# Top-32 attention and a capacity-limited mixture of experts: rearranging both ends of the kernel

## The chip, the cores and the metric

The kernel runs on one core of one Trainium2 chip. The metric is the device time of one execution in microseconds; lower is better. The core has a matrix engine (PE, with its weight loads shown as PEld), a vector engine (DVE), a scalar engine (ACT), a general engine (POOL), a queue that only issues transfers (SP), and sixteen DMA engines. Each engine works through its own list of instructions in order and waits on semaphores for the others. PE writes its results to PSUM, eight banks of 128 x 512 fp32; the other data lie in SBUF, and inputs and outputs in DRAM.

## The reference

Attention over 8 batches, 8 heads, 576 positions and head size 64, where each row of scores keeps its 32 largest entries; its output, as 4608 tokens of 512 numbers, goes through eight experts, each token to the one with the largest logit, and each expert keeps the 80 tokens with the largest gate.

```python
def _attn_ref(q, k, v):
    scores = scale * np.matmul(q, k.transpose(0, 1, 3, 2))
    kth = np.partition(scores, -top_k, axis=-1)[..., -top_k:-top_k + 1]
    scores = np.where(scores >= kth, scores, -1000000000.0)
    attn = np.exp(scores - np.max(scores, axis=-1, keepdims=True))
    attn = attn / (np.sum(attn, axis=-1, keepdims=True) + 1e-09)
    return np.matmul(attn, v)

def _moe_ref(x, w_gate, w1, w2, capacity):
    logits = x @ w_gate
    expert_idx = np.argmax(logits, axis=1)
    probs = softmax(logits)
    gate_w = probs[np.arange(N), expert_idx]
    out = np.zeros((N, D))
    for e in range(E):
        tok_idx = np.where(expert_idx == e)[0]
        if len(tok_idx) > capacity:
            keep = np.argpartition(-gate_w[tok_idx], capacity)[:capacity]
            tok_idx = tok_idx[keep]
        h = np.maximum(x[tok_idx] @ w1[e], 0.0)
        out[tok_idx] = gate_w[tok_idx, None] * (h @ w2[e])
    return out
```

Sizes of the second part: w1 is 8 x 512 x 1024, w2 is 8 x 1024 x 512.

## The kernel before

**Attention.** Work comes in 32 pairs of heads (`n`). `load` brings a pair's q, k and v; `turn` transposes q and k on PE (ten transposes into the four-bank score tile `sp`, which `four()` hands out and of which there is only one) and ACT copies the two halves to `qT` and `kT` (L189). A pair has five tiles of rows (`t`), four of 128 rows and a last one of 64 in which both heads share the partitions. A *unit* is one tile of one head: nine units a pair, 288 in all. For a tile, `front` multiplies q by k into `sp` (L201) and ACT copies the scores to `s` (L206). For a unit, DVE searches the 32nd largest score of every row: `parts` takes maxima of six stretches (L213), `search` takes maxima of those (L224, L232), ACT counts signs against the 24th (L229), DVE or, for odd units, POOL multiplies scores by signs (L236), DVE takes another maximum (L238) and picks the threshold (L241). `below` makes a mask (L250 on ACT, L254 on POOL or, for the last unit, DVE). `turn_w` transposes scores and adds masks on PE into `ab` (two banks, one buffer) and `cc` (L286, L291), and ACT takes the exponentials into `wT` (L293, L295). `back` multiplies by v (L309), `over` takes reciprocals of the sums (DVE, L321), `divide` scales into `xn` (ACT, L330).

**The order.** `run` writes the order out by hand: `step(i)` interleaves the searches of units i to i-4, then `turn_w` of the tile ended by unit i-4, the divisions, `front` of the tile that begins with unit i+4, `back` of the tile ended by unit i-5, and, where no front was issued, `turn` of the next pair. Steps run from -4 on.

**After a pair.** `norm` writes `xn` to DRAM (`xd`, two transfers, L336 and L337), transposes it into a score tile (L178, L179), copies it to `xT` (L342), multiplies it by the gate's weights in another score tile (twenty small matmuls, L347), copies the 40 logits of each row out (L353) and adds them up over the four pairs of a batch (L356). After every second batch `gates` makes the gate weights on DVE (L367 to L390) into `R`. `norm` is a generator: each `yield` puts its next part into a later step.

**Routing.** `route` first makes fixed matrices on POOL and DVE (L597 to L625: `emask`, `same`, `ahead`, `ofe`, `ones`, `col`, `base`). Then it transposes `R` (L637), takes the 24 largest of each group (L647 to L657), merges them (L653), searches the 80 largest of each expert (L669, L671), and builds lists of tokens with PE (`acc`, L701). `warm(n)` issues n idle 128x128 by 256 bf16 matmuls on zeros (L632): 100 after the merge (WARM1), 36 after `acc` (WARM2).

**Experts.** `finish` loads the weights of expert 4, calls `route`, makes two lists of indices on DVE (`idx_x` for reading, L722, `idx_s` for writing, L725 and L727), and runs eight experts in a pipeline. `gather` reads 80 rows of `xd` by an indirect DMA of POOL (L740), `turn_g` transposes them (L750, copied by DVE, L752), `hidden` makes the hidden layer (128 matmuls, L763, two copies with ReLU on ACT, L765), `product` multiplies by w2 (128 matmuls in one PSUM bank `yp`, L776, copied by ACT after each half, L779), `store` transposes back (L785), scales (DVE, L787) and writes rows to `out` by an indirect DMA of POOL (L788). In round e the order is `hidden(e)`, `store(e-2)`, `product(e-1)`, loads of weights, `gather(e+3)`, `turn_g(e+2)`. `judge` checks that the fast search was exact; otherwise a second, plain path would run, which it does not here.

Of the kernel before, what the change touches and what calls it, by code (L numbers as in the profile page):

```python
# [11 lines left out]
I32 = mybir.dt.int32  # L12
# [15 lines left out]
def kernel(  # L28
# [33 lines left out]
    WARM1, WARM2 = 100, 36  # L62
# [40 lines left out]
    nc.scalar.mul(huge, ident, -HUGE)  # L103

# [22 lines left out]
    class Attention:  # L127
# [47 lines left out]
        def turn_in(self, ps, t):  # L175

            for c in range(NF):
                nc.tensor.transpose(ps[:, c * P : (c + 1) * P], t[:, c, :], ident)  # L178
            nc.tensor.transpose(ps[:, NF * P : S], t[:TL, NF, :], ident[:TL, :TL])  # L179

        def turn(self, n):

            four = self.four()
            ps = [four[:, 2 * j : 2 * j + 2, :].rearrange("p j c -> p (j c)") for j in range(2)]
            for j, src in enumerate(self.qk.pop(n)):
                self.turn_in(ps[j], src.rearrange("p c h d -> p c (h d)"))
            self.turned[n] = [self.qkp.tile([P, S], F32, name=name, tag=name) for name in ("qT", "kT")]
            for j in range(2):
                nc.scalar.copy(self.turned[n][j], ps[j][:, :S])  # L189

        def front(self, n, t):
# [14 lines left out]
            nc.scalar.activation(s[:, : g * S].rearrange("p (j c) -> p j c", c=HS), ps[:, : 2 * g, :HS], Act.Copy, scale=TINY)  # L206
# [67 lines left out]
        def turn_w(self, n, t):  # L274
# [3 lines left out]
            ab = self.ps_w.tile([P, 2, NF, P], F32, name="ab", tag="ab")  # L278
# [53 lines left out]
        def norm(self, n, b, hp, bi, nb):  # L332

            xn = self.xn.pop(n).rearrange("p c h d -> p c (h d)")
            ones, cols = bass.ds(b, 1), slice(hp * P, (hp + 1) * P)
            nc.sync.dma_start(xv[ones, : NF * P, cols].rearrange("o (c p) d -> p (o c) d", p=P), xn[:, :NF, :])  # L336
            nc.sync.dma_start(xv[ones, NF * P :, cols].rearrange("o p d -> p o d"), xn[:TL, NF:, :])  # L337
            yield 1
            ps = self.four()[:, :2, :].rearrange("p j c -> p (j c)")
            self.turn_in(ps, xn)  # L340
            xT = self.xT
            nc.scalar.copy(xT[:, :S], ps[:, :S])  # L342
            yield 1
            lp = self.four()[:, 0, : NK * E].rearrange("p (c e) -> p c e", e=E)
            for c in range(NK):
# [5 lines left out]
            lg = self.lg[:, bi]  # L351
            part = lg if hp == 0 else self.small.tile([P, NK, E], F32, name="part", tag="part", bufs=2)
            nc.scalar.copy(part, lp)  # L353
# [3 lines left out]
            if hp == HP - 1 and bi == nb - 1:  # L357
                yield 0
                yield from self.gates(b - bi, nb)
# [527 lines left out]
```

## Time and profile before

| | us |
|---|---|
| median of 7 runs | 1028.66 (1027.07 to 1030.61) |
| the profiled execution | 1027.55 |
| its span, first to last instruction | 1025.8 |
| busy: PE, DVE, ACT, POOL | 899.4, 895.5, 786.1, 456.0 |
| attention, first search of DVE to last maximum | 12.3 to 880.5 |
| last pair's sums, gates | 880.5 to 893.7 |
| routing up to the first gather | 893.7 to 920.0 |
| experts | 924 to 1025.8 |

The profile gives, for each engine, busy time by source line and output tile, the idle time ahead of a group of instructions and what ended it, the clock that PE was granted (1.0 is full, 0.5 is half), and the chain of waits that ended last. L286 means line 286 of the kernel before. In a timeline a row has the start, the length, the engine, the line, the operation, the output and inputs, and in brackets the idle time of that engine just before, with what released it.

### The profile page before, as it was taken

The page shows a single profiled execution, that of the slowest core. Times are in us where ns is not written, and L with a number is a line of the kernel's source. Part 1 is how long each engine was busy: PE and PEld are TensorE (multiplying, and loading weights), DVE is VectorE, ACT ScalarE, POOL GpSimd, SP SyncE. Part 2 cuts the span into 40 slices and gives each one's busy share as a digit, 9 for nine tenths or more (in the row PEclk, how much of TensorE's full clock was granted, in tenths as well). Part 3 has the DMA queues.
Part 4 walks back from the last instruction along what each step waited for, and adds up shares of the span by engine and source line. Part 5 has one row for each costly group of instructions (what it writes and reads, how often), then busy time and mean ns, then how long its engine had stood idle before and what let it go on. Part 6 is the DMA issues. An engine that isn't in the chain of part 4 may idle for free.

```text
span 1025.8 us, 35579 instructions
## 1 busy us (share of the span) xinstructions
PE 899.4 (88%) x13381; PEld 727.0 (71%) x13381; DVE 895.5 (87%) x5087; ACT 786.1 (77%) x1671; POOL 456.0 (44%) x331
## 2 busy tenths in 40 slices
PE   5889999999889999989899999998989998699896
PEld 3677777777667777777677777776777777588786
DVE  3999999999999999999999999999999999551000
ACT  3888899888888998889898888898889888401110
POOL 1544555554454545545454544555455554211101
PEclk9999999999999999999999999999999999879998
DMA  4244443333333333332333311111121200225900
GB/s 93 77 118 130 122 128 89 89 89 89 90 89 87 73 79 79 79 84 81 89 89 89 89 40 44 40 47 48 48 49 48 49 13 14 96 89 201 352 23 24
DMA packets 167893, 85.76 MB, mean 84 GB/s; under 512 B 117792, under 2 KB 154656, under 8 KB 167712
## 3 DMA queue, kind: packets, MB, share of 16 engines
q1 hardware_dynamic: 166688, 80.78, 28.8%
q0 software_dynamic: 1024, 2.62, 0.9%
q8 instruction: 107, 1.75, 0.7%
q14 instruction: 74, 0.61, 0.2%
HBM read 63.19 MB, written 20.19 MB: 81 GB/s over the span
## 4 chain that ended last, share of the span: by engine, by line
DVE 55%; PE 28%; ACT 11%; issue 3%; another core or an unknown queue 1%; DMA 1%; POOL 0%; SPq 0%; POOLq 0%; ACTq 0%; DVEq 0%
DVE cand L213 17%; DVE w L238 12%; PE cc L309 7%; DVE y L236 6%; DVE cand L232 6%; DVE pick L241 4%; DVE top L224 4%; PE yp L776 3%; PE ab L286 3%; PE sp L201 3%; ACT wT L295 3%; PE sp L178 2%; ACT sign L229 2%; DVE w L224 2%; ACT mask L250 1%
## 5 line engine op out<-in xcount | busy, mean ns | idle before, releaser
L213 DVE MAX8 cand<-s 128x8 f32<-128x96 f32 x1728 | 386.7, 243 | 9.5 <-ACT s L206 9.5
L254 POOL TENSOR_SCALAR mask<-s,thr_all 128x576 bf16<-128x576 f32 x159 | 273.7, 1721 | 199.7 <-PE ab L291 135.2
L309 PEld LDWEIGHTS cc<-vb,wT 128*64 128x64 f32 x5760 | 200.3, 138 | 112.6 <-ACT wT L295 95.7
L236 POOL TENSOR_TENSOR y<-s,sign 128x576 f32<-128x576 f32 x128 | 164.0, 1281 | 240.3 <-ACT sign L229 106.4
L309 PE MATMUL cc<-vb,wT 128*64 128x65 f32 x5760 | 222.4, 225 | 53.1 <-ACT wT L295 53.1
L229 ACT ACTIVATE sign<-s,w 128x576 bf16<-128x576 f32 x288 | 225.9, 785 | 46.5 <-DVE w L224 46.2
L238 DVE MAX8 w<-y 128x8 f32<-128x576 f32 x288 | 217.3, 755 | 2.2 <-POOL y L236 2.0
L201 PE MATMUL sp<-kT,qT 64*128 64x288 f32 (+1 forms) x1280 | 202.0, 435 | 14.7 <-ACT part L353 6.1
L286 PE MATMUL ab<-ident,s 128*128 128x128 f32 x1152 | 176.7, 282 | 10.9 <-ACT wT L295 10.9
L206 ACT ACTIVATE s<-sp 128x1152 f32<-128x1152 f32 (+1 forms) x160 | 167.2, 1045 | 11.1 <-PE sp L201 9.5
L286 PEld LDWEIGHTS ab<-ident,s 128*128 128x128 f32 x1152 | 128.5, 142 | 34.6 <-ACT wT L295 25.1
L295 ACT ACTIVATE wT<-ab 128x1024 f32<-128x1024 f32 (+1 forms) x160 | 150.8, 942 | 0.0
L201 PEld LDWEIGHTS sp<-kT,qT 64*128 64x128 f32 (+1 forms) x1280 | 105.5, 179 | 53.3 <-ACT part L353 8.0
L236 DVE TENSOR_TENSOR y<-s,sign 128x576 f32<-128x576 f32 x160 | 118.2, 739 | 3.1 <-ACT sign L229 2.6
L224 DVE MAX8 top<-cand 128x8 f32<-128x48 f32 x576 | 114.2, 198 | 0.1
L291 PEld LDWEIGHTS <-mask 128*128 128x128 bf16 x1440 | 94.5, 98 | 25.7 <-ACT mask L250 19.0
L232 DVE MATCH_REPLACE8 cand<-top,cand 128x48 f32<-128x48 f32 x576 | 109.8, 191 | 0.0
L250 ACT ACTIVATE mask<-s,thr_all 128x576 bf16<-128x576 f32 x128 | 99.5, 777 | 0.3 <-DVE pick L241 0.2
L330 ACT ACTIVATE xn<-cc,z_all 128x64 f32<-128x64 f32 (+1 forms) x320 | 82.8, 316 | 2.3 <-DVE z_all L321 2.3
L241 DVE SCALAR_TENSOR_TENSOR pick<-past,cnt,w 128x9 f32<-128x9 f32 x288 | 82.7, 287 | 0.0
L286 PE MATMUL cc<-ident,s 128*128 128x128 f32 x288 | 79.0, 274 | 0.2 <-ACT xn L330 0.2
L293 ACT ACTIVATE wT<-cc 128x256 f32<-128x256 f32 (+1 forms) x160 | 57.5, 359 | 6.3 <-PE cc L291 4.8
(192 smaller groups left out, 978.1 us busy)
## 6 DMA issues: line engine op xcount, KB each, us to landing
w<-in_moe_w_dram SPq DMA_DIRECT2D x32, 512.0 KB, 4.6
w<-in_moe_w_dram SPq DMA_DIRECT2D x8, 2048.0 KB, 12.5
out_dram<-zero SPq DMA_DIRECT2D x9, 1024.0 KB, 5.9
qn<-in_q_dram SPq DMA_DIRECT2D x64, 128.0 KB, 2.6
kn<-in_k_dram SPq DMA_DIRECT2D x64, 128.0 KB, 2.5
vb<-in_v_dram SPq DMA_DIRECT2D x64, 128.0 KB, 2.6
xd<-xn SPq DMA_DIRECT2D x32, 256.0 KB, 4.2
qn<-in_q_dram SPq DMA_DIRECT2D x32, 32.0 KB, 2.5
```

The lines of the kernel that those rows point to most:

```text
L201: nc.tensor.matmul(o, lhsT=qT[d, t * P : t * P + m], rhs=kT[d, j * HS : (j + 1) * HS], start=True, stop=True)
L206: nc.scalar.activation(s[:, : g * S].rearrange("p (j c) -> p j c", c=HS), ps[:, : 2 * g, :HS], Act.Copy, scale=TINY)
L213: nc.vector.max(out=cand[:, j, :], in_=s[:, j * S // NG : (j + 1) * S // NG])
L224: nc.vector.max(out=dst, in_=cand)
L229: nc.scalar.activation(sign, s, Act.Sign, bias=w9[:, 7:8], scale=-1.0, accum_out=cnt)
L232: nc.vector.match_replace(out=cand, in_to_replace=dst, in_values=cand, imm_value=LOW)
L236: engine.tensor_tensor(out=y, in0=s, in1=sign, op=Alu.mult)
L238: nc.vector.max(out=w9[:, 8:], in_=y)
L254: engine.tensor_scalar(self.mask[i], self.s[i], self.thr[:, i : i + 1], None, op0=Alu.is_lt)
L286: nc.tensor.matmul(dst[h][c], lhsT=sc[:, keys[c]], rhs=ident, start=c == 0 or (c == NF and h == 0), stop=False, is_transpose=True, skip_gr ...
L295: nc.scalar.activation(wT[:, : g * NF, :], ab.rearrange("p h c r -> p (h c) r")[:, : g * NF, :], Act.Exp, scale=scale / TINY)
L309: nc.tensor.matmul(cc[r : r + TL, o], lhsT=wT[:, j * NF + c if c < NF else 2 * NF + j, r0 : r0 + TL], rhs=vb[:, c, h, :], start=(c == 0), ...
```

## The change

The diff, cut to its core; the plain path's buffers (`route_all`) become fewer, which changes nothing that runs.

1. The numbers of idle matmuls go from 100 and 36 to 92 and 14.
2. Fixed matrices are made at the kernel's beginning; `ofe` is dropped, a part of `same` takes its place.
3. `turn` writes one tile for q and k. For the first pair q is copied before k is transposed; for the others one copy moves both.
4. The first tile's scores are copied one head at a time. In steps 0 and 1 `front` looks three units ahead and not four, and the second pair's `turn` isn't allowed in step 0.
5. The last `turn_w` puts its `ab` into the score tile.
6. The last pair goes through `norm` twice, first with four chunks of rows, then with the fifth. The steps in which `norm` no longer waits for a free place begin one step earlier.
7. The buffers of the experts and the PSUM of `turn_g` and `store` are set aside before routing instead of after it. `idx_s` is made after the first three gathers are issued.
8. `product` is copied once as a whole; the last expert's is copied by halves, from two PSUM tiles.

```diff
-    WARM1, WARM2 = 100, 36
+    WARM1, WARM2 = 92, 14
...
+    GB = 2 * B
+    GE = B * E
+    emask = const.tile([P, E], F32, name="emask")
+    nc.vector.tensor_reduce(emask, ident.rearrange("p (g e) -> p e g", e=E), axis=AX, op=Alu.add)
+    same = const.tile([P, GB, E], F32, name="same")
+    nc.vector.tensor_copy(same, emask.unsqueeze(1).to_broadcast([P, GB, E]))
+    ahead = const.tile([P, P], F32, name="ahead")
+    nc.gpsimd.affine_select(out=ahead, in_=same.rearrange("p g e -> p (g e)"), compare_op=Alu.is_gt, fill=0.0, base=0,
+                            pattern=[[1, P]], channel_multiplier=-1)
+    for i in range(2):
+        nc.gpsimd.memset(base[i * GE : (i + 1) * GE, 1:2], float(2 * P if i == 0 else TL // 2))
+    nc.gpsimd.iota(base_i, pattern=[[0, 1]], base=0, channel_multiplier=1)
+    nc.vector.tensor_scalar(base_i, base_i, 3, None, op0=Alu.arith_shift_right)
+    nc.vector.tensor_copy(base[:, 0:1], base_i)
...
+            both = self.qkp.tile([P, 2, S], F32, name="both", tag="both")
+            self.turned[n] = both[:, 0, :], both[:, 1, :]
             for j, src in enumerate(self.qk.pop(n)):
                 self.turn_in(ps[j], src.rearrange("p c h d -> p c (h d)"))
-            self.turned[n] = [self.qkp.tile([P, S], F32, name=name, tag=name) for name in ("qT", "kT")]
-            for j in range(2):
-                nc.scalar.copy(self.turned[n][j], ps[j][:, :S])
+                if n == 0:
+                    nc.scalar.copy(both[:, j, :], ps[j][:, :S])
+            if n > 0:
+                nc.scalar.copy(both, four.rearrange("p (k j) c -> p k (j c)", k=2)[:, :, :S])
...
-            nc.scalar.activation(s[:, : g * S].rearrange("p (j c) -> p j c", c=HS), ps[:, : 2 * g, :HS], Act.Copy, scale=TINY)
+            for j in range(0, 2 * g, 2 if i == 0 else 2 * g):
+                w = 2 if i == 0 else 2 * g
+                nc.scalar.activation(s[:, j * HS : (j + w) * HS].rearrange("p (j c) -> p j c", c=HS), ps[:, j : j + w, :HS],
+                                     Act.Copy, scale=TINY)
...
-            ab = self.ps_w.tile([P, 2, NF, P], F32, name="ab", tag="ab")
+            if i == NU - 1 and not self.lean:
+                ab = self.four().rearrange("p h (c r) -> p h c r", r=P)
+            else:
+                ab = self.ps_w.tile([P, 2, NF, P], F32, name="ab", tag="ab")
...
-        def norm(self, n, b, hp, bi, nb):
+        def norm(self, n, b, hp, bi, nb, cs=range(NK)):
...
+            if full:
+                nc.sync.dma_start(xv[one, : NF * P, cols].rearrange("o (c p) d -> p (o c) d", p=P), xn[:, :NF, :])
+            if NF in cs:
+                nc.sync.dma_start(xv[one, NF * P :, cols].rearrange("o p d -> p o d"), xn[:TL, NF:, :])
             yield 1
             ps = self.four()[:, :2, :].rearrange("p j c -> p (j c)")
-            self.turn_in(ps, xn)
+            at = slice(cs[0] * P, min(S, cs[-1] * P + P))
+            self.turn_in(ps, xn, cs)
-            nc.scalar.copy(xT[:, :S], ps[:, :S])
+            nc.scalar.copy(xT[:, at], ps[:, at])
             yield 1
             lp = self.four()[:, 0, : NK * E].rearrange("p (c e) -> p c e", e=E)
-            for c in range(NK):
+            for c in cs:
...
-                ends = [n for n, t in drawn if t == NF]
+                ends = [(n, range(NK) if n < NP - 1 else range(NF) if t < NF else range(NF, NK))
+                        for n, t in drawn if t == NF or (n == NP - 1 and t == NF - 1)]
...
-                busy = 0 <= i + 4 < NU and units[i + 4][2] != 1
+                f = i + 4 if i not in (0, 1) else i + 3
+                busy = 0 <= f < NU and units[f][2] != 1
                 if busy:
-                    self.front(*units[i + 4][:2])
+                    self.front(*units[f][:2])
...
-                if due and not busy:
+                if due and not busy and i > 0:
...
-                    step(i, i >= NU + 6)
+                    step(i, i >= NU + 5)
...
-            nc.tensor.matmul(few[:, 0:1], lhsT=ofe.rearrange("k g e -> k (g e)"), rhs=bar8, start=True, stop=True)
+            nc.tensor.matmul(few[:, 0:1], lhsT=same[:E, :, :].rearrange("k g e -> k (g e)"), rhs=bar8, start=True, stop=True)
...
+        fs = stack.enter_context(tc.tile_pool(name="fs", bufs=2))
+        ps_x = stack.enter_context(tc.tile_pool(name="ps_x", bufs=2, space=PSUM))
         routing = stack.enter_context(ExitStack())
...
-            ps = ps_y.tile([P, HP, P], F32, name="yp", tag="y")
             y_t[e] = fs.tile([P, HP, cap], F32, name="yT", tag="yT")
+            step = HP if e < E - 1 else HP // 2
             for d in range(HP):
+                if d % step == 0:
+                    ps = ps_y.tile([P, HP, P], F32, name="yp", tag="y")
...
-                if d % 2:
-                    nc.scalar.copy(y_t[e][:, d - 1 : d + 1, :], ps[:, d - 1 : d + 1, :cap])
+                if d % step == step - 1:
+                    nc.scalar.copy(y_t[e][:, d + 1 - step : d + 1, :], ps[:, d + 1 - step : d + 1, :cap])
...
             for e in range(3):
                 gather(e)
+            em = sl.tile([cap, E], F32, name="em")
+            nc.vector.tensor_scalar(em, i1, 0.0, float(4 * N), op0=Alu.is_equal, op1=Alu.mult)
+            idx_s = sl.tile([cap, E], I32, name="idx_s")
+            nc.vector.scalar_tensor_tensor(out=idx_s, in0=i1, scalar=-1.0, in1=em, op0=Alu.add, op1=Alu.add)
```

## The prediction

> **What bounds the kernel now.** I read the 40 slices first, then stretches of 100 us, then the chain of waits through the end, then the timelines of the first 32 us and from 866 us on.
>
> ```profile
> DVE  3999999999999999999999999999999999551000
> PEclk9999999999999999999999999999999999879998
> 760.00:860.00 100.00, 90.53 (x1312) 72.10 (x1309) 100.00 (x581) 90.95 (x193) 50.83 (x34) 1.00 0.13 32
> ```
>
> The third line is one stretch of the attention (length, then busy us of PE, PEld, DVE, ACT, POOL, then clock): DVE is busy for all of it, PE and ACT for 91 of 100. So from 30 to 866 us the program is DVE's list, and an edit that spares ACT there (one copy in `turn` instead of two) moves nothing. The change can earn only where DVE is not full: the first 30 us, the drain from 866 to 894, the routing to 924, the experts to the end. The experts, by the chain of waits:
>
> ```profile
> 945.38 0.44 ACT hT L765
> 945.82 4.12 another core or an unknown queue
> 949.97 0.30 ACT yT L779
> 950.27 0.04 issue
> 950.32 2.43 PE yp L776 x64
> ...
> 984.94 2.56 PE yp L776 x64
> 987.58 0.30 ACT yT L779
> ```
>
> Between the halves of each product PE stands still for ACT's copy of the first half: both halves share one PSUM tile. For experts 1, 2 and 3 the copy is released late as well: 4.12, 4.08 and 4.04 us after the piece before, where other first halves take 2.24 to 2.57. POOL's timeline names the only thing special there, a scatter and a gather back to back; each late copy starts 0.7 to 0.8 us after that pair ends:
>
> ```profile
> 947.04 0.95 POOL L788 DMA_INDIRECT out_dram<-y,idx_s  x1 [20.24 <-DVE y L787]
> 948.29 0.97 POOL L740 DMA_INDIRECT xg<-xd,idx_x  x1 [0.30 <-issue]
> ```
>
> **Experts.** Eight products, first yp matmul to the next other matmul: 5.14, 6.78, 6.85, 8.18, 5.41, 5.25, 5.42, 5.41, together 48.44 us. `hidden` runs the same 128 matmuls (64 at a time, 128x80 out) without a stop in 4.42 us (930.64 to 935.06), 4.58 when a transpose follows. Eight at 4.58, one of them at 4.42, are 36.5, so 11.9 us go. Within it, 1.45 is a clock drop in expert 3 (below), about 1.5 each is the late release of experts 1 to 3 (4.4), the rest the plain stop, 0.6 to 0.85 a product. The last expert keeps half copies but in two PSUM tiles, so it loses its stop too. The whole copy is 320 columns; the row of that size is L765, 0.44 us, against 0.29. It hides behind the next transposes and `hidden` (5 us before `store` reads yT), except in the last round, where `store(6)` follows `product(6)` directly: now 0.97 us from matmul to matmul (two transposes overlap the second copy), then about 0.26+0.44+0.04+0.56 = 1.30. Cost 0.3. Sum: -11.6. If the late release is not tied to POOL and PE only waits elsewhere, 4.4 and the clock drop stay: -5.7.
>
> **Drain.** The last turn of weights (L286, unit 287) waits for ACT to empty `ab`:
>
> ```profile
> 883.88 0.66 PE L286 MATMUL ab<-ident,s 128*128 128x128 f32 x4 [1.23 <-ACT wT L295]
> 888.58 0.64 ACT L342 COPY xT<-sp 128x576 f32<-128x576 f32 x1 [0.36 <-PE sp L179]
> 891.62 0.38 DVE L598 TENSOR_REDUCE emask<-ident 128x8 f32<-128x128 f32 x1 [0.23 <-POOL base L619]
> ```
>
> In the score tile, free since 876.74, it starts at 882.5 and ends at 883.5, under that copy; the 60 matmuls of L309 then start at 883.88 instead of 884.86: -1.0. The chunks cost part of it. ACT still does the last division first, then the four chunks' copy of xT; then come 16 logit matmuls and a copy (0.6 and 0.2), and only when that copy has freed the single score tile may the fifth chunk be transposed, copied, multiplied and copied again (0.3, 0.2, 0.25, 0.2 with 0.04 to 0.05 between): 3.45 us from L309's end to `lg`, now 3.04. +0.4. Queued behind that wait are PE's last two logit products, and all of routing waits for them. The second write of `xd` is the same two DMAs on SP (256 and 32 KB), a little earlier, 30 us before the first gather: nothing. Moving the fixed matrices takes emask (0.38, its 0.23 wait) and four small DVE rows (0.14 to 0.15, partly in the shadow of others) out of the gates: 891.39 to 893.75 shrinks from 2.36 to about 1.66, -0.7. At the beginning they cost nothing: POOL idles 21.05 us before 24.17 and DVE 9.11 before 12.30, against 0.7 and 1.5 us of work; PE's first transposes wait for q until 3.94, not for POOL. Without that cover it would be those 1.5 us. Drain: -1.3, bounds 0 (chunks cost all of the 1.0, the matrices were hidden) and -2.1 (chunks free).
>
> **Gather.** idx_x is done at 918.99, idx_s at 919.25, the first gather starts at 919.98, said to wait for idx_s. Bounds: 0 (POOL's own start-up, 0.7) and -0.9 (all from 918.99 but 0.1). I take -0.3, the difference of the two.
>
> **Clock.** Columns: PE busy second, granted clock third from the end.
>
> ```profile
> 914.74:918.16 3.42, 3.42 (x29) 3.42 (x28) 0.00 (x0) 0.00 (x0) 0.00 (x0) 0.50 0.00 0
> 918.16:921.57 3.41, 3.41 (x20) 2.47 (x20) 0.57 (x4) 0.00 (x0) 1.28 (x2) 0.50 0.00 0
> 921.57:924.98 3.41, 3.18 (x32) 2.71 (x30) 0.49 (x1) 0.00 (x0) 2.24 (x3) 1.00 0.50 132
> 972.77:976.18 3.41, 1.39 (x41) 1.23 (x38) 0.00 (x0) 0.29 (x1) 1.16 (x2) 1.00 0.45 133
> 976.18:979.60 3.42, 3.42 (x51) 3.25 (x46) 0.00 (x0) 0.29 (x1) 0.00 (x0) 0.50 0.02 5
> ```
>
> A stretch with PE 41% busy was followed by one at half clock, where 64 yp matmuls took 3.79 us instead of 2.43; the 36 idle matmuls after `acc` ran through the half-clock stretch from 918.16 and brought the clock back. Fourteen of them, at 0.213 us each while cold, last 3.0 us and end about 3 us before `hidden(0)`. If the clock is then at half, it comes back after one or two stretches of dense matmuls (3.4 to 6.8 us), which lose half: 1.7 to 3.4 us. Bounds 0 and +3.4; I take +2.0, near the short end. WARM1 at 92 ends 1 us earlier, under DVE's search: nothing.
>
> The Trainium skill speaks against this edit (TensorE: Matmul & The Clock Gate, "Part 1: The HAM clock gate"): full clock needs about 3.4 us of sustained activity in a free-running window. These windows agree (3.41 us). By the rule 3.0 us never fill one, and the sum would carry 2.6 for the clock instead of 2.0.
>
> **Beginning.**
>
> ```profile
> 7.57 0.64 ACT L189 COPY qT<-sp 128x576 f32<-128x576 f32 x1 [4.94 <-PE sp L179]
> 12.30 1.06 DVE L213 MAX8 cand<-s 128x8 f32<-128x96 f32 x6 [9.11 <-ACT s L206]
> 20.09 0.76 DVE L236 TENSOR_TENSOR y<-s,sign 128x576 f32<-128x576 f32 x1 [2.64 <-ACT sign L229]
> ```
>
> The copy of qT waits for all ten transposes. Placed before kT's it runs while k arrives; kT's copy then starts at 7.57 and `front(0)` at 8.27 instead of 8.80: -0.5 on PE. With scores copied by halves (0.64 each, 0.53 apart) DVE starts at 11.3, a microsecond sooner, but PE's next front starts only 0.5 sooner. Moving the third front one step later, and the turn of pair 1 two, puts ACT's first sign ahead of the third copy of scores and the second ahead of pair 1's copies, so the 2.64 us stall goes, with most of the 2.04 at 25.48 that waits for POOL. DVE is then up to 3 us ahead, while the cold row of front, copy, front, copy, turn is only 0.5 ahead. What is late next is the score tile of pair 1: its sign, then POOL's y, which before was ready 0.36 us ahead of DVE (36.39 against 36.75). DVE stalls there until it is 0.5+0.3 = 0.8 ahead, and keeps that. Bounds 0 and -3.0; I take -0.8.
>
> **Sum.** -11.6 -1.3 -0.3 +2.0 -0.8 = -12.0 us. The profiled execution took 1027.55 (span 1025.8 and 1.75 around it) and would come to 1015.5; the median lies 1.11 higher at 1028.66, which carries over: **1016.6**. What a measurement can tell from no change is 0.2%, 2.1 us.
>
> **Rivals.**
> - *The late release stays* (1022.5): the 1.5 us of experts 1 to 3 belong to the loads of weights running then (DMA share 1.03 from 948.88 to 952.29), and PE stalls elsewhere; 4.4+1.45 come back. For: only these three are late. Against: other waits of PE and ACT in the same stretch are on time.
> - *All of the beginning, no clock lost* (1012.5): -3.0 for -0.8 and 0 for +2.0, so 4.2 lower. For: ACT and PE have 9% to spare once the clock is up. Against: POOL's 0.36 us.
> - *The change does not do what it says* (1028): PE stops for the whole copy as long as for two halves, because what follows needs it. Only `store(6)` is such a place.
> - *The clock stays at half into the experts* (1030.2): 128 matmuls then take 8.84 instead of 4.42. Without the clock the sum is -14.0; three experts at half, some 31 us, give back 15.5. It decides from 28 us at half clock on. For: PE enters cold. Against: no dense stretch of this trace stayed at half longer than 6.8 us.
>
> **Chances.** Forecast 0.52 (its own range 1013.5 to 1020); late release 0.17; all of the beginning 0.24; nothing 0.03; half clock 0.04. Faster 0.93, same 0.03, slower 0.04. The unknown costs added at their good ends give 1010 (-11.6 -2.1 -0.9 -3.0), at their bad ends 1026 (-5.7 +3.4); 8 in 10 lie between 1011 and 1022.5, which takes in the first two rivals.
>
> **What would show it.** No wait of yp for yT but in the last expert, products at 4.4 to 4.6 us, no unknown queue in the chain; the last L286 before 883 in today's time and the fifth chunk's transposes behind a copy of `part`; the clock at 0.50 in the first expert; DVE's first maximum near 11.3, later a stall on POOL's y. Wrong: products above 5 us, or DVE idle inside the attention after 45 us.

## The result, and the profile after

| | before | after |
|---|---|---|
| median | 1028.80 us (46 runs) | 1021.01 us (19 runs) |
| profiled execution | 1027.55 | 1020.83 |
| its span | 1025.8 | 1019.1 |
| mean granted clock | 0.984 | 0.981 |

The ratio is 0.9914, 95% interval 0.9905 to 0.9924: 0.9% faster, 7.8 us, where 12.0 were forecast. In later sets of runs the kernel of before itself took 1022.5 us, and the gain was smaller there; that is part of the answer and comes below. Line numbers from here on are those of the changed kernel (products L789, their copy L792, the last turn of weights L318, division L362, hidden layer L774).

The middle of the kernel is untouched. First the two rows of the 40 slices that were shown of before,

```profile
DVE  5899999999999999999999999999999999661110
PEclk9999999999999999999999999999999999977999
```

and the stretch of the attention:

```profile
760.00:860.00 100.00, 90.55 (x1307) 72.07 (x1307) 99.99 (x580) 90.86 (x190) 50.96 (x34) 1.00 0.13 32
```

DVE begins earlier (5 and 8 in the first two slices instead of 3 and 9), is full up to the drain, and PE, DVE and ACT are as busy as before in the 100 us. The profiled executions differ by 6.7 us of span. Dividing them at five rows that both have tells where:

| stretch | before | after | difference | forecast |
|---|---|---|---|---|
| start to the 285th `w<-y` of DVE | to 871.35 | to 871.47 | +0.1 | -0.8 |
| to the first transpose of R | to 893.75 | to 892.44 | -1.4 | -1.3 |
| to idx_x | 25.07 | 26.12 | +1.05 | in the clock's |
| to the first gather | 1.16 | 0.47 | -0.69 | -0.3 |
| to expert 2's transposes | 10.24 | 12.30 | +2.06 | +2.0, the clock's |
| to the end | 95.6 | 87.8 | -7.8 | -11.6 |

**The experts.** The chain of waits, in order of time (start, length, what):

```profile
947.15 2.78 PE yp L789 x76
949.93 0.34 issue
950.27 0.42 PE yp L789 x5
950.69 0.34 issue
951.03 1.88 PE yp L789 x47
...
981.15 4.58 PE yp L789 x128
```

The wait for ACT's copy and the "unknown queue" are gone. Product 4 (the last row) runs its 128 matmuls in one piece in 4.58, as forecast. Products 1 to 3 don't: PE stops twice for 0.34, waiting for nothing that the profile shows, and restarts slowly (5 matmuls in 0.42, where a dense run takes 0.18). From the first yp matmul to the next other matmul the eight take 5.20, 5.76, 5.77, 5.77, 4.58, 4.48, 5.23, 4.58, together 41.4 (before 48.5); the 5.23 of product 6 holds 0.63 in which `store(6)` waits for the one large copy. On POOL's timeline stands the same pair as before, beside the stops:

```profile
948.22 0.95 POOL L801 DMA_INDIRECT out_dram<-y,idx_s  x1 [22.61 <-DVE y L800]
949.47 0.97 POOL L751 DMA_INDIRECT xg<-xd,idx_x  x1 [0.31 <-issue]
```

The second stop ends at 951.03, 0.59 us after the gather (950.44). Before, the late release came 0.7 after it. So what made the copies late is still there and now takes PE's time in another form.

**The drain.** PE and ACT around the last turn of weights:

```profile
881.59 0.60 PE L318 MATMUL sp<-ident,s 128*128 128x128 f32 x4
...
882.81 0.52 ACT L362 ACTIVATE xn<-cc,z_all 128x64 f32<-128x64 f32 x2
...
883.38 0.33 PE L318 MATMUL cc<-ident,s 128*128 128x128 f32 x1 [1.19 <-ACT xn L362]
```

Four transposes go into the score tile `sp` at 881.59, early as intended. The fifth needs `cc`, which has two buffers; the older is empty only when ACT has divided out of it, at 883.3. PE idles 1.19, and `back` starts 4.04 us after the tile before was turned, against 4.07. The chunks cost 0.47 from the last sums to `lg`, and without the matrices `lg` to `cd_ps` takes 2.61 instead of 3.45. That sums to -0.4; the other -1.0 of the stretch is the phase of the clock, which was at half for 6.8 us here before (866.96 to 873.78) and for 3.4 after (868.00 to 871.41). Variants from below that keep the changed kernel's drain show that size. From DVE's 286th `w<-y` to the first transpose of R, five profiled executions with 3.4 us at half take 17.85 to 17.97 us, the two with 6.8 us (loads left out, all gathers first) 18.88 and 18.87. The drain of before takes 19.28 with 6.8 us, and 18.12 with 3.4 us from 868.89 on (before with whole copies alone). At the same clock the change gains 0.3 to 0.4 there. (Where the 3.4 us lie later, 873.61 to 877.02 in before once more, they cost as much as the 6.8: 19.44.)

**The clock.** Columns: PE busy second, granted clock third from the end.

```profile
908.95:912.37 3.42, 2.33 (x21) 1.87 (x20) 2.34 (x11) 0.00 (x0) 0.00 (x0) 1.00 0.00 0
912.37:915.78 3.41, 3.41 (x29) 3.41 (x28) 0.00 (x0) 0.00 (x0) 0.00 (x0) 0.50 0.00 0
915.78:919.19 3.41, 3.41 (x26) 3.10 (x26) 0.57 (x4) 0.00 (x0) 0.16 (x1) 0.50 0.00 0
919.19:922.61 3.42, 2.44 (x12) 1.52 (x11) 0.00 (x0) 0.00 (x0) 2.81 (x3) 0.50 0.28 73
922.61:926.02 3.41, 2.91 (x34) 2.50 (x34) 0.98 (x2) 0.00 (x0) 2.04 (x3) 0.50 0.38 119
926.02:929.44 3.42, 3.42 (x58) 3.42 (x55) 0.00 (x0) 0.43 (x1) 0.00 (x0) 0.50 0.20 53
929.44:932.85 3.41, 3.41 (x90) 3.23 (x88) 0.49 (x1) 0.45 (x2) 0.00 (x0) 1.00 0.14 22
```

The clock falls in the middle of `acc` (912.37, before 914.74) and is back only at 929.44 (before 921.57): by these rows PE was busy for all of the first two windows at half, for 71 and 85% of the next two and for all of the fifth, and only the fifth was followed by full clock; before, the second full one was. So `acc` is 1 us longer and the first hidden layer takes 7.0 instead of 5.3.

**The beginning.** DVE's first row, and the waits that follow it:

```profile
11.86 1.06 DVE L241 MAX8 cand<-s 128x8 f32<-128x96 f32 x6 [8.26 <-ACT s L233]
...
29.04 0.76 DVE L266 MAX8 w<-y 128x8 f32<-128x576 f32 x1 [1.81 <-POOL y L264]
...
36.78 0.76 DVE L266 MAX8 w<-y 128x8 f32<-128x576 f32 x1 [1.60 <-POOL y L264]
```

The stall of 2.64 behind the first sign is gone and DVE is 2.6 us ahead at 18.24 (20.89 before); then it waits twice for POOL's `y`, and at 36.78 it is where it was before (36.75). One thing in this execution is not the edits': the first transfers of q are issued at the same time (0.81 and 0.82), but PE can start on q only at 4.58, before at 3.94.

### The profile page after: what moved, and what is told of

Same layout as the page of the kernel before. It is cut to its first block, busy times and chain, and to the rows that moved or that the text cites. A ratio compares the mean times of both kernels' runs of the same rounds, so it can differ in the third digit from the quotient of the medians.

```text
span 1019.1 us, 35489 instructions
## 1 busy us (share of the span) xinstructions
PE 899.9 (88%) x13351; PEld 727.4 (71%) x13351; DVE 895.8 (88%) x5089; ACT 783.9 (77%) x1636; POOL 455.5 (45%) x329
## 3 DMA queue, kind: packets, MB, share of 16 engines
q0 software_dynamic: 1024, 2.62, 0.8%
q8 instruction: 107, 1.75, 0.7%
## 4 chain that ended last, share of the span: by engine, by line
DVE 74%; PE 19%; ACT 3%; issue 2%; DMA 1%; POOL 0%; POOLq 0%; SPq 0%; ACTq 0%; DVEq 0%
DVE cand L241 24%; DVE w L266 17%; DVE y L264 9%; DVE cand L260 9%; DVE pick L269 5%; DVE top L252 5%; PE yp L789 4%; PE cc L341 3%; DVE w L252 2%; PE sp L226 2%; PE ab L318 2%; DVE z_all L353 1%; PE warm L649 1%; ACT wT L327 1%; ACT sign L257 1%
## 5 line engine op out<-in xcount | busy, mean ns | idle before, releaser
L226 PE MATMUL sp<-both 64*128 64x288 f32 (+1 forms) x1280 | 202.0, 435 | 14.1 <-ACT part L391 6.1
L318 PE MATMUL ab<-ident,s 128*128 128x128 f32 x1148 | 176.2, 282 | 9.6 <-ACT wT L327 9.6
L318 PEld LDWEIGHTS ab<-ident,s 128*128 128x128 f32 x1148 | 128.1, 142 | 33.2 <-ACT wT L327 23.7
L226 PEld LDWEIGHTS sp<-both 64*128 64x128 f32 (+1 forms) x1280 | 105.5, 179 | 52.8 <-ACT part L391 8.0
L362 ACT ACTIVATE xn<-cc,z_all 128x64 f32<-128x64 f32 (+1 forms) x320 | 82.3, 313 | 2.6 <-DVE z_all L353 2.3
L318 PE MATMUL cc<-ident,s 128*128 128x128 f32 x288 | 79.1, 275 | 1.4 <-ACT xn L362 1.4
L323 PE MATMUL ab<-minus,mask 128*128 128x128 bf16 x636 | 61.6, 220 | 0.0
```

What stands on the lines that cost most here:

```text
L226: nc.tensor.matmul(o, lhsT=qT[d, t * P : t * P + m], rhs=kT[d, j * HS : (j + 1) * HS], start=True, stop=True)
L318: nc.tensor.matmul(dst[h][c], lhsT=sc[:, keys[c]], rhs=ident, start=c == 0 or (c == NF and h == 0), stop=False, is_transpose=True, skip_gr ...
```

## The experiments

Ten variants, and both kernels once more, in three sets; every ratio is to the kernel of before on the chip of its set. They ran on chips numbered 9, 14 and 11. The kernel of before took 1028.8 us in the first set and 1022.5 and 1022.6 in the second and third. Whether the chips differ or only their condition, nothing here tells; medians are compared within a set only.

| set | kernel | median us | ratio, 95% interval |
|---|---|---|---|
| 1 | loads of experts 5 to 7 left out | 1019.11 | 0.9906, 0.9891 to 0.9921 |
| 1 | all gathers first | 1026.13 | 0.9959, 0.9944 to 0.9974 |
| 1 | copies by halves again | 1028.45 | 0.9995, 0.9984 to 1.0006 |
| 1 | idle matmuls of before | 1019.72 | 0.9911, 0.9896 to 0.9926 |
| 2 | gather apart from scatter | 1023.73 | 1.0010, 0.9998 to 1.0021 |
| 2 | last cc in another tile | 1018.37 | 0.9960, 0.9946 to 0.9974 |
| 2 | beginning of before | 1020.69 | 0.9982, 0.9972 to 0.9993 |
| 2 | before, with whole copies alone | 1020.77 | 0.9984, 0.9975 to 0.9993 |
| 3 | before once more (one run) | 1023.67 | |
| 3 | the changed kernel once more | 1019.27 | 0.9969, 0.9957 to 0.9980 |
| 3 | cc in another tile, gates in one piece | 1017.46 | 0.9953, 0.9938 to 0.9968 |
| 3 | cc in another tile, idle matmuls of before | 1018.23 | 0.9959, 0.9945 to 0.9973 |

### Copies by halves again (first set)

```diff
-            step = HP if e < E - 1 else HP // 2
...
-                if d % step == 0:
-                    ps = ps_y.tile([P, HP, P], F32, name="yp", tag="y")
+            ps = ps_y.tile([P, HP, P], F32, name="yp", tag="y")
...
-                if d % step == step - 1:
-                    nc.scalar.copy(y_t[e][:, d + 1 - step : d + 1, :], ps[:, d + 1 - step : d + 1, :cap])
+                if d % 2:
+                    nc.scalar.copy(y_t[e][:, d - 1 : d + 1, :], ps[:, d - 1 : d + 1, :cap])
```

> The changed kernel with the product copied by halves out of one tile, as before. Theory, the gain of the change is the experts' alone: products 4 to 7 take 5.3 to 5.4 us, 1 to 3 take 6.8 (late copy of the first half), the time goes back by 7 to 8 us, to 1028.5. Rival, part of the 7.8 us comes from elsewhere (drain, gather) and the copies by halves cost only what PE stands in products 4 to 7 (0.8 us each, eight times): 1021 + 6.4 - 0.4 = 1027. A time under 1025 speaks against both.

1028.45 against 1028.83: with this one part undone the whole gain is gone. The other parts, together, are worth nothing that shows (the interval leaves 1.6 us of gain to 0.6 of loss). The late release is back, in the chain of waits of product 1 (and alike in 3):

```profile
948.86 4.14 another core or an unknown queue
953.00 0.02 issue
953.02 0.30 ACT yT L790
```

Products 4 to 7 take 5.43, 5.33, 5.43, 5.41, and 0 to 3 take 6.99, 8.43, 6.84, 8.22. Products 0, 1 and 3 hold more than the late release: a stop of 1.57 at 938.96, of a kind that comes below, and a clock at half from 953.40 to 956.82 and from 980.71 to 984.12. This execution was the slowest of the ten.

### Who stops PE in products 1 to 3: the loads or POOL? (first set)

```diff
                     if 5 <= e + 4 < E:
-                        for dma in load_w(e + 4, wpool):
-                            dma()
+                        w1_t[e + 4], w2_t[e + 4] = w1_t[e], w2_t[e]
```

> The changed kernel with the loads of experts 5, 6 and 7 left out (they compute with the weights of experts 1, 2 and 3; the output of these three experts is therefore another one, the instructions of every engine but SP are the same). Theory A, PE's stops inside products 1 to 3 (two of 0.34 us each, product 5.77 us against 4.58 in products 4 to 7) come from the weights that are loading: products 1 to 3 take 4.6 us, the kernel takes 1021 - 3.5 = 1017.5. Theory B, they come from POOL's scatter and gather back to back; theory C, from PE's own stream of instructions: in both products 1 to 3 stay at 5.8 us and the time at 1021.

Products 1 to 3 stay at 5.69, 5.66, 5.66, with the two stops at the same place as with the loads (the chain of waits):

```profile
945.73 2.84 PE yp L789 x77
948.57 0.29 issue
948.86 0.43 PE yp L789 x6
949.28 0.34 issue
949.63 1.79 PE yp L789 x45
```

So the weights that are loading are not the cause: theory A falls, and with it the cause that the prediction's first rival gave. The median of 1019.1 lies between the two expectations; what it gains on 1021 is within the interval. One thing did go: the stop of 0.39 in product 0 (now 4.53).

```diff
-            for e in range(3):
+            for e in range(E):
                 gather(e)
...
-                if e + 3 < E:
-                    gather(e + 3)
```

The gathers 3 to 7 get five buffers of their own.

> The changed kernel with all eight gathers issued ahead of the first expert, so that no gather follows a scatter later. Theory B, POOL's pair stops PE: products 1 to 3 take 4.6 us, the time is 1021 - 3.5 = 1017.5. Theory A, the weights that are loading stop it, or C, PE's own stream: products 1 to 3 stay at 5.8, the time at 1021.

Product 1 has no gather beside it now and takes 4.58 in one piece; product 3 takes 4.92. The stops went where the gathers went. PE's timeline while POOL issues gathers 3 to 7 (up to 930 us), in the first hidden layer:

```profile
924.96 1.74 PE L775 MATMUL hp__17184<-xt,w 128*64 128x80 f32 x43
927.02 0.36 PE L775 MATMUL hp__17184<-xt,w 128*64 128x80 f32 x4 [0.33 <-issue]
928.46 0.36 PE L775 MATMUL hp__17184<-xt,w 128*64 128x80 f32 x4 [1.08 <-issue]
929.19 0.23 PE L775 MATMUL hp__17184<-xt,w 128*64 128x80 f32 x1 [0.37 <-issue]
```

That layer takes 11.4 us; its stops (with two more, 0.49 and 0.87) are 3.1 of it, and from 929.65 on the clock is at half. The kernel of before agrees: after two gathers back to back (924.58 and 925.84) PE stops for 0.31 in its first hidden layer, up to 927.38, 0.58 after the second. For the first set theory B is shown: where gathers follow a scatter or each other on POOL, PE stands. How POOL's transfers reach PE, neither run says. The time, 1026.13, is neither theory's: besides that layer, products 0 and 2 became longer, and for another reason:

```profile
963.20 0.35 PE yp L790 x5
963.55 3.21 issue
966.76 1.26 PE yp L790 x21
```

PE waits 3.21 us here with no gather near (one scatter starts in the middle of it). (The rest of product 2's 9.71 is a clock at half, 967.19 to 970.61.) It stands before its 24257th recorded instruction (matmuls, weight loads and the waits of PE's queue, counted from the start), and in product 0, for 1.25 us, before the 23233rd. The difference is 1024, four times 256. In every kernel, the stops between experts 0 and 4 that neither indirect transfers back to back nor a wait for another engine explains stand at such counts: 23233, 24001, 24257, 24513, 24769 or 25025, all 193 above a multiple of 256. Instructions arrive in blocks of 16384 bytes, by transfers that the trace lists on a queue of their own. PE's count when each of them started:

```
no loads, first set        22985 23233 23494 23746 23987 24245 24511 24776 25023
changed kernel, first set  23137 23295 23490 23868 24115 24409 24629 24929 25051
changed kernel, third set  23113 23295 23490 23878 24199 24503 24727 24814 25036
```

The edges near are 22977, 23233, 23489 and so on. Without the loads the next fetch starts within 14 instructions of each edge. With them it starts up to 160 late on the same chip and up to 246 in the third set (24503 for the edge at 24257), and PE may reach the next edge first. In the run with the stop of 3.21 the fetch that without the loads starts near 24001 (23987) starts only at 964.41, when PE has stood at 24257 since 963.55. So theory C holds too, for other stops than the pairs', and here the loads are the cover under which it happens; that the large stops of the second and third sets would vanish without loads was not tried. The Trainium skill (Runtime: NRT & Kernel Launch, "Instruction fetch mechanics") has blocks of 256 instructions, fetched ahead by the engine's own transfers and mostly hidden. The 256 agree; "hidden" doesn't, where the weights load: 3.21 us above.

### Gather apart from scatter (second set)

```diff
-            xg_t[e] = fs.tile([cap, Dm], F32, name="xg", tag="xg", bufs=3)
+            xg_t[e] = fs.tile([cap, Dm], F32, name="xg", tag="xg", bufs=2)
...
                 if e + 2 < E:
                     turn_g(e + 2)
+                if e + 4 < E:
+                    gather(e + 4)
```

The gathers 2 and 3 stand behind the first two `turn_g` in the same way.

> The changed kernel with two buffers for gathered rows instead of three and each gather behind the transposes that free its buffer: in a round it then starts at the end of the round, some 3 us after the scatter, not right behind it. Theory B, a scatter and a gather back to back on POOL hold PE up, one alone doesn't: products 1 to 3 take 4.6 us instead of 5.77, no stop takes their place in the next hidden, 1021 - 3.5 = 1017.5. Rival, every indirect transfer of rows holds PE up for 0.3 to 0.6 us: products 1 to 3 lose one stop each and the next hidden gains one, the time stays within 1 us of 1021.

1023.73, no faster than before (1.0010, and the interval takes in 1); the changed kernel was not run in this set. It can't decide between its theories: in this set and the next the pair doesn't stop PE in any kernel, so there was nothing to gain. All its stops stand at edges of blocks: 0.85, 1.75, 1.07, 2.23 us between two instructions, at 23233, 24257, 24513 and 24769.

### Before with whole copies alone (second set), and both kernels once more (third set)

> The kernel of before with the whole copies of the product alone. Theory, since the changed kernel with copies by halves is as slow as before, the whole copies are the entire gain: 1028.8 - 7.8 = 1021, products 4 to 7 at 4.6 us and 1 to 3 at 5.8. Rival, the copies earn less without the other edits, because the clock's return is earlier there and the gather later: 1023 or more.

1020.77, the theory's number for the wrong reason: before was at 1022.5 there and not at 1028.8, so the gain is 1.7 us, not 7.8, and the products take 4.64, 4.91, 5.94, 6.38, 4.58, 4.48, 5.23, 4.58. Why the kernel of before was itself faster there had to be seen in its profile:

> The kernel of before once more, for its profile on the chip of this call: in the second set of runs it took 1022.5 us where it took 1028.8 in the first. Theory, the chips differ in the experts: where the kernel takes 1022.5, the copies of experts 1 to 3 are not late, these three products take 5.4 us instead of 6.8 to 8.2. Rival, the difference lies in the attention (DVE, the transfers) or the clock, and the late copies are there in both: products 6.8 and more at 1022.5.

Product 1 of before, in its chain of waits in the third set, and POOL's timeline beside it:

```profile
947.25 2.39 PE yp L776 x64
949.64 0.02 issue
949.67 0.30 ACT yT L779
949.97 0.04 issue
950.01 2.43 PE yp L776 x64
```

```profile
948.32 0.95 POOL L788 DMA_INDIRECT out_dram<-y,idx_s  x1 [19.55 <-DVE y L787]
949.57 0.97 POOL L740 DMA_INDIRECT xg<-xd,idx_x  x1 [0.30 <-issue]
```

No unknown queue: the copy starts 2.42 after the product's first piece, not 4.15. PE's signal is there 0.26 us after the half's last matmul begins, where it took 1.83 to 1.86 in the first set, with POOL's pair in the same place. The products take 5.14, 5.19, 5.79, 5.25, 5.25, 5.14, 5.25, 5.25, together 42.3 against 48.5; these 6.2 us are the whole difference between the two medians of before (6.2 to 6.3). Another mark tells the sets apart: a load of weights of 2 MB lands after 10.1 us (median) here and 15.5 there.

> The changed kernel once more, timed and profiled beside the kernel of before on this chip. Where before takes 1028.8: 1021, products 1 to 3 at 5.8 us, two stops of 0.34 in each. Where before takes 1022.5: theory, what is left of the experts' gain is the plain stop less the stops that PE's late instruction blocks bring (1020.5, as its version with the old beginning took 1020.7 there); rival, the gain is 7.8 everywhere: 1014.7.

1019.27 and 0.9969, near the theory's 1020.5. Products 1, 3 and 4 take 4.58, and PE waits at edges of blocks elsewhere, as in the hidden layer of expert 4:

```profile
963.00 1.39 issue
964.39 2.36 PE hp__17728 L774 x62
```

Four such stops, 0.31, 0.70, 1.67 and 1.41 from start to start of PE's instructions, come to 4.1; before has three in this set (1.27, 0.50, 0.41), 2.2. (The profile puts the last of the four down to ACT's hT, which had been done for 0.85.) From expert 2's transposes to the end this kernel takes 87.5, before 90.5: the gain in the experts is 3.0 here and 7.8 in the first set.

### The clock (first set)

```diff
-    WARM1, WARM2 = 92, 14
+    WARM1, WARM2 = 100, 36
```

> The changed kernel with the idle matmuls of before (100 and 36 instead of 92 and 14). Theory, fourteen idle matmuls leave the clock at half into the first expert: with 36 the clock is back before hidden(0), which takes 5.3 us or less instead of 7.0, the time is 1021 - 2 = 1019. Rival, the drop and the return go by where the grid of 3.41 us windows happens to lie, not by the number of idle matmuls: the time stays at 1021, some executions with hidden(0) at 7.

In the profile the theory's step is there: the clock is full from 920.74, the first hidden layer takes 5.2, and from the first transpose of R to expert 2's transposes it is 36.6 us instead of 38.9. Of that, the median has 1.3 (1019.72), and the ratios, 0.9911 and 0.9914, can't be told apart. One row speaks for the rival: the first gather starts 1.7 earlier (917.31), and expert 0's rows are transposed no sooner (922.4, changed kernel 922.3), since the 36 idle matmuls still run. Of the nine profiled executions with 14 idle matmuls seven have the clock at half into the first hidden layer, which takes 6.8 to 7.1 us; with all gathers first it is back at 922.82, ahead of that layer, and with cc in another tile and gates in one piece at 920.25 (the layer takes 4.58):

```profile
913.42:916.83 3.41, 3.41 (x28) 3.35 (x28) 0.03 (x1) 0.00 (x0) 0.00 (x0) 0.50 0.00 0
916.83:920.25 3.42, 2.92 (x14) 1.75 (x12) 0.55 (x4) 0.00 (x0) 2.17 (x3) 0.50 0.18 48
920.25:923.66 3.41, 2.21 (x44) 1.97 (x46) 0.98 (x2) 0.00 (x0) 2.77 (x3) 1.00 0.43 123
```

There the clock had fallen earlier, at 910.01, and it came back after a full window and one of 85%. The changed kernel's rows, two full ones without a return, show that this can't be read off the busy share. All five with 36 have the clock back ahead of the layer, which takes 5.3 or less. So the number of idle matmuls shifts the odds, against the rival; what decides in a single execution isn't shown.

### The last cc (second set)

```diff
                 ab = self.four().rearrange("p h (c r) -> p h c r", r=P)
+                cc = self.ps_w.tile([P, 2, NF, P], F32, name="ab", tag="ab").rearrange("p h c r -> p (h c r)")[:, :512]
             else:
                 ab = self.ps_w.tile([P, 2, NF, P], F32, name="ab", tag="ab")
-            cc = self.ps_c.tile([P, 512], F32, name="cc", tag="cc")
+                cc = self.ps_c.tile([P, 512], F32, name="cc", tag="cc")
```

> The changed kernel with the last cc in the tile where the last ab stood before, so that it needn't wait for the division to empty one of cc's two buffers. Theory, the 1.0 us forecast for the score tile was lost to that wait: from the third back group to the last one 4.04 us become 3.0 (1.0 less), the wait of 1.19 behind ACT's xn is gone, and the time falls by 1.0, less than the interval shows. Rival, the exp of the last unit or the copy of xT ahead of it sets the last back group: it stays at 4.0 us.

The wait behind the division is gone, but another stands in its place (the tile is called `ab` here, and is freed by the exp of the tile before):

```profile
882.46 0.33 PE L319 MATMUL ab<-ident,s 128*128 128x128 f32 x1 [0.78 <-ACT wT L328]
```

0.78 instead of 1.19: `back` comes 3.63 after the tile before was turned, not 4.04. That is 0.4, not 1.0; neither side of the expectation had it. The median is 2.3 below that of the kernel with the old beginning. Of the 1.3 between their profiled spans (1018.6 and 1019.9) the drain accounts for 0.5 and the stretch ahead of it, where the two beginnings differ, for 0.6 (DVE's 286th `w<-y` at 874.13 and 874.75).

### The beginning of before (second set)

```diff
-                if n == 0:
-                    nc.scalar.copy(both[:, j, :], ps[j][:, :S])
-            if n > 0:
-                nc.scalar.copy(both, four.rearrange("p (k j) c -> p k (j c)", k=2)[:, :, :S])
+            for j in range(2):
+                nc.scalar.copy(both[:, j, :], ps[j][:, :S])
...
-            for j in range(0, 2 * g, 2 if i == 0 else 2 * g):
-                w = 2 if i == 0 else 2 * g
+            for j in range(0, 2 * g, 2 * g):
+                w = 2 * g
...
-                f = i + 4 if i not in (0, 1) else i + 3
+                f = i + 4
...
-                if due and not busy and i > 0:
+                if due and not busy:
```

> The changed kernel with the beginning of before (both copies of pair 0 after all transposes, the scores of unit 0 in one copy, fronts four units ahead, pair 1 turned one step sooner). Theory, the first 32 us earn nothing, because pair 1's y on POOL takes back what DVE gains: DVE is at the same row at 36.8 us within 0.2, time 1021. Rival, the edits there are worth the 0.8 forecast and something else of the profiled run hid it: 1021.8, and DVE's row at 36.8 comes 0.8 later.

DVE has its old waits again,

```profile
12.34 1.06 DVE L239 MAX8 cand<-s 128x8 f32<-128x96 f32 x6 [8.75 <-ACT s L231]
...
20.14 0.76 DVE L262 TENSOR_TENSOR y<-s,sign 128x576 f32<-128x576 f32 x1 [2.64 <-ACT sign L255]
25.52 0.76 DVE L264 MAX8 w<-y 128x8 f32<-128x576 f32 x1 [2.03 <-POOL y L262]
```

and reaches the row of 36.78 at 36.87, the 101st row of that kind at 321.41 (changed kernel 321.52, before 321.12). As the theory said, against this execution of the changed kernel: 0.1. But q was there at 3.94 here and at 4.58 there. In the five profiled executions with the changed beginning in which q was there by 4.03, the second front starts at 11.72 to 11.87 (here 12.36, before 12.32), the row of 36.78 at 35.30 to 36.55 (36.75 to 37.08 in the three with the old beginning and q by 3.94), and the 101st row at 320.63 to 320.99 in four of them (322.69 in the fifth; 321.12, 321.41 and 322.11 with the old one). So the edits gain where q is early, and a late q takes that back; the pair above doesn't show that they are worth nothing. The medians don't settle it: 0.9982 here and 0.9969 for the changed kernel in the third set have intervals that overlap, and they are from two sets.

### Two combinations (third set)

"Gates in one piece" takes the chunks of the last pair back:

```diff
-                ends = [(n, range(NK) if n < NP - 1 else range(NF) if t < NF else range(NF, NK))
-                        for n, t in drawn if t == NF or (n == NP - 1 and t == NF - 1)]
+                ends = [(n, range(NK)) for n, t in drawn if t == NF]
...
-                    step(i, i >= NU + 5)
+                    step(i, i >= NU + 6)
```

> The changed kernel with the last cc in a tile of its own and the last pair's gates in one piece, as before. Theory, the chunks cost 0.4 us and the wait for cc 1.0: 1.4 less than the changed kernel on the same chip. Rival, with cc apart the chunks pay, since the first four can go ahead of the last division: 0.5 less than the changed kernel.

From the last `back` to the last row of `lg` it takes 5.63 us, with chunks 6.07 or 6.08 in every kernel but one (gather apart, 6.19) and 5.64 in before: the chunks cost 0.44 also where `cc` is apart. It was the fastest kernel of all, 1.8 under the changed kernel of its set, theory 1.4; the intervals of the two overlap, so only its lead on before (0.47%) is certain.

> The changed kernel with the last cc in a tile of its own and the idle matmuls of before (100 and 36). Theory, 1.0 for cc and 1.3 for the clock (the difference of the first set's medians): 2.3 less than the changed kernel on the same chip, the fastest so far. Rival, the idle matmuls keep the first expert's transposes waiting for as long as the clock gains: 1.0 less.

1.0 under the changed kernel: the rival's number, but the two intervals (1.4 and 1.2 us to either side) take in the theory's 2.3 as well. In the profiles the first hidden layer takes 4.58 instead of 7.10. What the clock gives back is too small for these medians to show.

## Why the prediction was right, and where it was not

The direction and the mechanism held: PE stood between the halves of a product, one copy instead of two took that away, and every other part together came to nothing that shows. The wide range, 1011 to 1022.5, held as well, but 1021.0 lies outside the forecast's own 1013.5 to 1020 and nearer to the first rival's 1022.5 than to 1016.6. The prediction's own sign of being wrong, products above 5 us, came for products 0 to 3 and 6. (The good ends of its terms add to 1011 from the median; its 1010 starts from the profiled execution.)

- **Experts, -11.6.** Its terms fared differently. The plain stop was right to 0.1: products 4, 5 and 7 went from about 5.4 to 4.5 or 4.58. The 1.45 of a clock drop in expert 3 did go. `store(6)` lost 0.4, forecast 0.3. The step that failed is "about 1.5 each is the late release of experts 1 to 3 (4.4)", taken as removed together with the copy that was late. Only 0.8 of it went: 3 x 1.19 = 3.6 us stay, as stops of PE beside POOL's scatter and gather. The place was named, with 0.7 us from the pair's end, and the rival "the late release stays" said that PE would stall elsewhere; but that rival put it to the loads of weights, and taking these away changed nothing. Another 0.6 stayed in product 0, of which 0.39 is a stop at the edge of a block of instructions, a cost that the prediction did not have. A signal that comes late needs to be asked what holds it, and whether that holds only the signal.
- The same term has no fixed size. In the third set there was no late release to remove, and PE, no longer stopped between halves, lost 4.1 us at late blocks of instructions where before lost 2.2. There the experts gained 3.0.
- **Drain, -1.3.** The size came out, by luck of the clock's phase (-1.0). The step "the 60 matmuls then start at 883.88 instead of 884.86: -1.0" failed: it looked at the release of `ab` alone, while the same `turn_w` also writes `cc`, which ACT's division frees. Gained: 0.03. The chunks (+0.4, measured +0.47 and 0.44) and the matrices (-0.7, measured -0.84) were right.
- **Gather, -0.3.** POOL did most of what the bound allowed: -0.69 of -0.9.
- **Clock, +2.0.** Mechanism right, size 3.1 in the profiled pair (2.06 up to expert 2 and 1.05 in `acc`, which the forecast did not expect to lose). Undoing it returned 2.3 in the profile and 1.3 in the medians.
- **Beginning, -0.8.** +0.1 in the profiled pair. There "PE's next front starts only 0.5 sooner" did not come: q arrived 0.64 later than before, k's transposes waited for q's copy (0.73), and the second front began at 12.42, against 12.32 before. Where q came as early as before, it did come (11.72 to 11.87), and DVE was 0.2 to 1.5 ahead of 36.75 at that row; the size of the term is open. POOL's `y` of the second pair, which the prediction named, is what DVE waits for.

The sum repeated with the measured terms: 0.1 - 1.4 + 1.05 - 0.69 + 2.06 - 7.8 = -6.7, the difference of the spans. Against the forecast's -12.0 that is 3.8 less in the experts, 1.1 more lost to the clock and 0.9 less at the beginning, with 0.5 to the good in gather and drain.

## What to carry to other kernels

When a wait goes away, ask what made it long as well as what made it be there: the cause of the excess may remain and take its time elsewhere. A tile moved to free storage gains only if every tile that the same instructions write is free too. And time one change on more than one chip: the same two kernels were 7.8 us apart in one set and 3.3 in another.

## What the runs showed of the hardware

- Beside a scatter and a gather back to back on POOL (0.95 and 0.97 us), PE's signal took 1.83 to 1.86 us instead of 0.26, or PE itself stopped twice for 0.34, on one chip (or in one condition of it), and not at all in the two later sets. Two gathers back to back stopped PE too, for 0.31.
- PE's instructions come in blocks of 256. While weights load (the DMA engines moved some 300 to 430 GB/s in the third set), a block's fetch begins late, by up to 246 instructions in the changed kernel. PE then may stand at the edge, for up to 3.2 us, mostly under "issue".
- The clock came back after a window that PE filled to 85% by the profile's modelled ends (916.83 to 920.25), and in another run did not come back after two full ones (912.37 to 919.19) nor after one of 85% (922.61 to 926.02): the busy share in such rows doesn't settle what brings the clock back.
